# Weight sums moved from VectorE to GpSimd, and a maximum and exponential placed four half units sooner, in a fused attention and two-MLP kernel

## The chip, the cores and the metric

One core of one Trainium2 chip. The metric is the device time of one execution in microseconds; the kernel is compared by the median of its runs.

## The reference

`q`, `k`, `v` are (8, 8, 576, 64) in float32: eight batches, eight heads, 576 positions.

```python
q_s = exp(q - max(q, axis=-1)); q_s = q_s / (sum(q_s, axis=-1) + 1e-09)
k_s = exp(k - max(k, axis=2));  k_s = k_s / (sum(k_s, axis=2) + 1e-09)
x = q_s @ (k_s^T @ v)                       # per head, then (4608, 512)
x = relu(x @ w_in)**2 @ w_out               # 512 -> 2048 -> 512, weights float64
xn = x / sqrt(mean(x*x) + 1e-6) * rms_g
out = (silu(xn @ w_gate) * (xn @ w_val)) @ w_out2   # 512 -> 1536 -> 512
```

## The kernel before

The 4608 tokens are cut into nine blocks of 512. Every large product is done as three TensorE passes over a rounded high part and a low part of each operand (`PASSES`), so each operand is split: ACT writes the high part, VectorE (DVE) subtracts it from the value to get the low part.

**Stages.** A start stage handles the attention of the first two batches. Then a loop runs over units `(j, c)`: block `j` from 0 to 6 and `c` from 0 to 15, a slice of 128 of the 2048 hidden columns. One unit computes `ps_h` (12 matmuls, `p1_A`), its relu and square (ACT), its split `w` (`p1_hi`, `p1_lo`) and, two units later, the second product into `acc` (12 matmuls, `p1_B`). The last two blocks, and the second MLP, are done later by a scheme of seven products for eight (`PROD`, `BPROD`, `p2_A`, `p2_V`), which needs sums and differences of quarters of the weights.

**Side work in the loop.** Beside the matmuls, the units of blocks 2 to 6 carry three kinds of work:

- *Weights of the second MLP.* `tick` (line 454) runs a pipeline per weight piece: load of the float64 words (`raw`), ACT's conversion (`d_words`), three DVE instructions that build the float32 (`d_float`). When the four quarters of a piece are there, `d_quad` (line 415) makes the sums `s1`, `s2`, `s3`, `s4` of 128x512 (tiles `s` in the profile's rows, from `t11` to `t22`, there `t`), and queues seven splits `so` (`d_out`, line 398), which are stored to DRAM.
- *Sums of the first MLP's weights.* `d_light` (line 369) rebuilds two weights in float32 (tiles `t`), and makes four sums of 128x256 in place (`t<-t`), and queues two splits `so`. This is done 16 times, once in four units.
- *Attention of batches 2 to 7.* It goes by pairs of heads `hp` 0 to 3 of a batch `j`. Transposed k, `kT`, has **one** buffer (line 500). `a_loadk` loads it, `a_kmax` (line 562) takes its maximum on DVE (`mc`) and copies it out (`mcb`, one buffer), `a_kes` (line 571) takes its exponential on ACT for the sum alone, after which the buffer is free for the next pair's load. `a_kb` transposes `mcb` on TensorE (`ps_kb`, in one of two PSUM banks that the attention takes in turn, `a_ps`, line 102), `a_ksub` adds it to k (`kt`, DVE), `a_kexp` writes `ke` (ACT), `a_kv` multiplies it with v (`ps_kv`, TensorE).

**What sets the order.** In this stretch the instructions of DVE, ACT, GpSimd and TensorE stand in the order in which the code calls them (`pinned`). The steps of the attention have a place in half units: `FIRST` (line 1392) for even `hp`, `SECOND` (line 1396) for odd `hp`; pairs 0 and 1 share a base, pairs 2 and 3 one that lies 16 half units later. `a_kmax` and `a_kes` stand at 2 and 3 in `FIRST`, at 4 and 5 in `SECOND`. `SOONER` and `LATER` shift a whole batch's half. The DMA loads go through the queue of SyncE (SP); where they stand among each other is worked out by the framework.

The queued weight work is run at the end of each unit (line 1642): `sums_l` holds `d_light`'s sums and splits, `outs` holds `d_quad`'s sums and splits.

```python
for queue, n in ((sums_l, 2), (outs, 1 if ticks[0] > before else 3)):
    for _ in range(min(n, len(queue))):
        queue.pop(0)()
```

Of the kernel before, what the change touches and what calls it, by code (L numbers as in the profile page):

```python
# [8 lines left out]
F32 = mybir.dt.float32  # L9
# [31 lines left out]
def attention_moe_kernel(  # L41
# [14 lines left out]
    ve, se, ge, te = (  # L56
        InOrder(tc, engine, pinned) for engine in (nc.vector, nc.scalar, nc.gpsimd, nc.tensor)
    )
    B, H, S, D = q.shape
    NT, DM = out.shape  # L60
    P = 128
# [113 lines left out]
    pools = {}  # L175
# [23 lines left out]
    def flat(t):  # L199
        return t.rearrange("p b f -> p (b f)").bitcast(F32)  # L200
# [5 lines left out]
    def ahead(j, key):  # L206

        return j == 1 and key[0] == "i" and key[1] in AHEAD
# [56 lines left out]
    def used(key):  # L265
        if key not in res1:
            wt.pop(key)
            used_up[0] += 1
            feed()
# [55 lines left out]
    def send(key, t, after):  # L325
        late.append([after, key, t])
# [39 lines left out]
    outs, lows, sums_l = [], [], []  # L366
    halves_l = {}

    def d_light(kind, j, c):
        n, r = divmod(c, 2)  # L370
        if (kind, j) not in (("i", 2 + n % 2), ("o", 4 + n % 2)):
            return
        t = pools["d"].tile([P, 512], U32, tag=f"t{r}", name="t", bufs=1).bitcast(F32)
        w = wt[kind, c].bitcast(F32)
        ve.tensor_tensor(out=t, in0=w[:, 0], in1=w[:, 1], op=ALU.add)
        halves_l[r] = t
        if r == 0:
            return
        f = [halves_l.pop(0), halves_l.pop(1)]
        half = [f[0][:, 0:HF], f[0][:, HF:], f[1][:, 0:HF], f[1][:, HF:]]  # L380
        a11, a12, a21, a22 = half if kind == "i" else (half[0], half[2], half[1], half[3])

        def sub(out, in0, in1, op=ALU.subtract):
            sums_l.append(lambda: ve.tensor_tensor(out=out, in0=in0, in1=in1, op=op))

        sub(a22, a21, a22, ALU.add)
        sub(a21, a11, a21)
        sub(a11, a22, a11)
        if kind == "i":
            d_out(("L", kind, 1, n), lambda: f[1], sums_l)  # L390
            sub(a12, a12, a11)
            d_out(("L", kind, 0, n), lambda: f[0], sums_l)
        else:
            d_out(("L", kind, 0, n), lambda: f[0], sums_l)
            sub(a12, a12, a11)
            d_out(("L", kind, 1, n), lambda: f[1], sums_l)

    def d_out(key, f, outs=outs):
        def run():
            t = pools["q"].tile([P, 2, 512], F32R, tag="so", name="so", bufs=5)  # L400
            src = f().rearrange("p (g f) -> p g f", g=2)
            ts = t.rearrange("p g (a f) -> p g a f", a=2)
            se.activation(out=ts[:, :, 0], in_=src, func=AF.Copy)

            def low():
                ve.tensor_tensor(
                    out=ts[:, :, 1], in0=src, in1=ts[:, :, 0].bitcast(F32), op=ALU.subtract
                )
                send(key, t, 0)

            lows.append(low)

        outs.append(run)

    def d_quad(key):
        n, c = key
        if n != "11":
            return
        f = {"a" + b: floats.pop((b, c)) for b in ("11", "12", "21", "22")}

        def d_sum(name, in0, in1, op):
            def run():
                f[name] = pools["q"].tile([P, 512], F32, tag=name, name=name, bufs=1)
                ve.tensor_tensor(out=f[name], in0=f[in0], in1=f[in1], op=op)

            outs.append(run)

        def out(name):
            d_out((name, c), lambda: f[name])

        d_sum("s1", "a21", "a22", ALU.add)
        d_sum("s3", "a11", "a21", ALU.subtract)
        out("a22")
        d_sum("s2", "s1", "a11", ALU.subtract)
        out("a11")
        out("s1")
        out("s3")
        d_sum("s4", "a12", "s2", ALU.subtract)
        out("s2")
        out("a12")  # L440
        out("s4")

    due = {}
    for c in range(FF1):
# [7 lines left out]
    ticks = [0]  # L452
# [293 lines left out]
    def a_kvd_hi(j, hp):  # L746
        if j < B:
            split_hi(kvs, (j, hp), kvd[j % 2][hp // 2][:, hp % 2])

    def a_kvd_lo(j, hp):  # L750
        if j < B:
            split_lo(kvs, (j, hp))
            kvs.pop((j, hp))
# [170 lines left out]
    def p1_h(j, c):  # L924
        ps = ps_h.tile([P, T], F32, tag="h", name="ps_h")
        for kk in range(KD):
            mm3(ps, wl(("i", c), kk), lambda b: xts[j, kk][:, b, :], kk == 0, kk == KD - 1)
        return ps
# [14 lines left out]
    def p1_A(j, c):  # L943
        if not ahead(j, ("i", c)):
            kept[j, c] = p1_h(j, c)
            d_light("i", j, c)
            if not (j == 0 and ahead(1, ("i", c))):
                used(("i", c))
# [5 lines left out]
    def p1_ahead_r(c):  # L954
        p1_r(1, c)

    def p1_hi(j, c):
        if not ahead(j, ("i", c)):
            p1_r(j, c)
        r = kept.pop((j, c))  # L960
        ghl[1, j, c] = r
        split_hi(ghl, (1, j, c), g_tile(c % 4))

    def p1_lo(j, c):
        split_lo(ghl, (1, j, c))
# [440 lines left out]
    for j in range(2, NB):  # L1406
        for hp in range(NP):
            for n, (at, f) in enumerate(SECOND if hp % 2 else FIRST):
                at += (j - 1) * 2 * FF1 - 4 + 4 * FF1 // NP * (hp // 2)
                at += SOONER.get((j, hp // 2), 0)  # L1410
                if f in (a_loadk, a_loadq, a_loadv):
                    at += LATER.get((j, hp // 2), 0)
                    if j == NB - 1:
                        at = U0 + (5, 6, 7, 10)[hp]
                todo.setdefault(at, []).append((-n, j, hp, f))
# [34 lines left out]
    with ExitStack() as ctx_a:  # L1450
# [24 lines left out]
        for j in range(2):  # L1475
# [7 lines left out]
            out=neg_r, in0=ident, scalar1=-1.0, scalar2=0.0, op0=ALU.mult, op1=ALU.add  # L1483
# [104 lines left out]
        def attention(at):  # L1588
            for n, j, hp, f in todo.get(at, ()):
                f(j, hp)  # L1590
# [4 lines left out]
        for i, (j, c) in enumerate(units[: JU * FF1]):  # L1595
            if i < EARLY:
                continue
            if i == 2 * FF1:
                ctx_r.close()
                ctx_k.close()  # L1600
                pools["q"] = ctx_q.enter_context(
                    tc.tile_pool(name="qp", bufs=1, reuse_waits="tile")
                )
            if i == (JU - 1) * FF1 + 8:
                assert not outs and not sums_l and ticks[0] == len(jobs) + 3
                flush(all=True)
                ctx_q.close()
                ctx_d.close()
                pools["y"] = ctx.enter_context(
                    tc.tile_pool(name="by", bufs=1, reuse_waits="tile", side="right")  # L1610
                )
            if j == 0:
                unit_of_0(c)
                if 8 <= c < 8 + NP:
                    a_kvd_hi(1, c - 8)
                    a_kvd_lo(1, c - 8)
                attention(2 * i)
                attention(2 * i + 1)
                continue
            p1_A(j, c)  # L1620
            for x in last:
                p1_hi(*x)
            if ticks[0] > NJ1 + 4:
                flush()
            if c == LAG:
                p1_out(j - 1)
            attention(2 * i)
            pending.append((j, c))
            while beside:
                p1_ahead_r(beside.pop())  # L1630
            while len(pending) > (LAG + 1 if j > 0 and c == LAG else LAG):
                p1_B(*pending.pop(0))
            for x in last:
                p1_lo(*x)
            last = [(j, c)]
            if j == 1 and 4 <= c < 4 + NTAG:
                key = res1[c - 4]
                tc.keep_in_program_order(nc.sync.dma_start(out=wd[key], in_=flat(wt[key])))
            before = ticks[0]
            while ticks[0] < n_ticks(i):  # L1640
                tick()
            for queue, n in ((sums_l, 2), (outs, 1 if ticks[0] > before else 3)):
                for _ in range(min(n, len(queue))):
                    queue.pop(0)()
            attention(2 * i + 1)
            while lows:
                lows.pop(0)()
# [68 lines left out]
        for op in plan2:  # L1716
            at = None
            if op[0] == "A":
                _, s, n, q = op
                pinned[0] = True  # L1720
                p2_A(s, n, q)
                at = n * 2 * NS + q
                if at in A_SPLITS:
                    f, m = A_SPLITS[at]
# [4 lines left out]
            else:  # L1729
                _, s, i, n = op  # L1730
                at = i * NQ + n
# [73 lines left out]
```

## Time and profile before

| what | value |
|---|---|
| median of 3 runs (lowest to highest) | 1692.53 us (1690.88 to 1695.87) |
| the profiled execution's own time | 1696.69 us |
| its span, first to last instruction | 1694.9 us |
| busy PE / PEld / DVE / ACT / POOL, us | 1654.3 / 1367.1 / 1219.8 / 894.5 / 24.7 |
| mean granted TensorE clock | 0.992 |
| DMA | 434.08 MB, 256 GB/s |

PE is TensorE's matmuls, PEld its weight loads, which run beside them, POOL is GpSimd, SP is SyncE, whose queue issues the loads. "a<-b,c" is an instruction that writes tile a from b and c. All instructions that the kernel's own recording layer issues have line 34. In a row of a timeline, the bracket at the end says how long the engine sat idle before, and what ended that.

### The profile page before, as it was taken

How to read it: one execution, taken by the hardware profiler on the slowest of the kernel's cores; microseconds unless marked ns; L12 is line 12 of the kernel's file. 1: busy time of each engine (PE TensorE's matmuls, PEld its weight loads, DVE VectorE, ACT ScalarE, POOL GpSimd, SP SyncE). 2: the span in 40 equal slices, each digit the busy share in tenths (PEclk: the TensorE clock that was granted, in tenths of full speed). 3: DMA queues.
4: the chain of work that ended last, by engine and by line, in shares of the span. 5: the costliest groups of instructions: out<-in, count | busy, mean ns of one | idle time of the engine just before them, and what ended most of it. 6: DMA issues, size and time to landing. Idle time of an engine off the chain costs nothing.

```text
span 1694.9 us, 23168 instructions
## 1 busy us (share of the span) xinstructions
PE 1654.3 (98%) x8190; PEld 1367.1 (81%) x8190; DVE 1219.8 (72%) x1936; ACT 894.5 (53%) x1462; POOL 24.7 (1%) x39
## 2 busy tenths in 40 slices
PE   6999999999998999999999999999999999999999
PEld 4888888787777787888788888888888888888898
DVE  7985467778778788546775678667866786668666
ACT  7875456656655666458744444344444444424433
POOL 5000000000000000000000000000000000000000
PEclk9999999999999999999999999999999999999999
DMA  8876988999998997656668666866686658665898
GB/s 264 313 285 243 296 265 301 329 368 341 335 320 275 332 357 261 244 196 189 186 205 276 189 186 208 277 188 190 203 275 195 191 183 269 194 188 197 242 388 301
DMA packets 205410, 434.08 MB, mean 256 GB/s; under 512 B 60784, under 2 KB 97648, under 8 KB 204144
## 3 DMA queue, kind: packets, MB, share of 16 engines
q1 hardware_dynamic: 178272, 369.82, 67.3%
q10 hardware_dynamic: 27024, 62.79, 9.7%
q8 instruction: 66, 1.08, 0.3%
q14 instruction: 48, 0.39, 0.1%
HBM read 347.08 MB, written 85.46 MB: 255 GB/s over the span
## 4 chain that ended last, share of the span: by engine, by line
PE 81%; DVE 6%; DMA 6%; ACT 5%; issue 1%; ACTq 0%; POOL 0%; POOLq 0%; SPq 0%; DVEq 0%
PE ps_x L34 22%; PE ps_y L34 18%; PE acc L34 12%; PE ps_h L34 12%; PE ps_v L34 10%; PE ps_w L34 5%; DMA kT<-in_k_t 2%; DVE t L34 2%; DMA ws<-wd_i 1%; DVE so L34 1%; ACT r L34 1%; PE ps_kv L34 1%; DMA kt<-in_k 1%; PE ps_q L34 1%; DVE w L34 1%
## 5 line engine op out<-in xcount | busy, mean ns | idle before, releaser
L34 PE MATMUL acc<-w,ws 128*128 128x512 f32 x1008 | 251.5, 399 | 0.0
L34 PE MATMUL ps_h<-x,ws 128*128 128x512 f32 x1008 | 247.9, 397 | 0.0
L34 PEld LDWEIGHTS acc<-w,ws 128*128 128x128 f32 x1008 | 190.9, 192 | 40.8 <-DVE w L34 0.5
L34 PEld LDWEIGHTS ps_h<-x,ws 128*128 128x128 f32 x1008 | 189.2, 190 | 40.1 <-ACT r L34 0.3
L34 PE MATMUL ps_y<-xo,ws 128*128 128x512 f32 (+1 forms) x816 | 194.3, 373 | 0.3 <-ACT sa L34 0.3
L34 PE MATMUL ps_v<-xo,ws 128*128 128x512 f32 (+1 forms) x816 | 194.0, 373 | 0.0
L34 PE MATMUL ps_x<-ob,ws 128*128 128x512 f32 x768 | 177.4, 389 | 0.0
L34 PE MATMUL ps_x<-xo,ws 128*128 128x512 f32 (+1 forms) x720 | 168.9, 370 | 0.0
L34 PEld LDWEIGHTS ps_y<-xo,ws 128*128 128x128 f32 x816 | 145.0, 188 | 29.2 <-ACT sa L34 0.8
L34 PEld LDWEIGHTS ps_x<-ob,ws 128*128 128x128 f32 x768 | 144.1, 188 | 30.0
L34 PEld LDWEIGHTS ps_v<-xo,ws 128*128 128x128 f32 x816 | 144.9, 188 | 28.7
L34 DVE TENSOR_TENSOR u<-ps_y,p 128x512 f32<-128x512 f32 (+1 forms) x136 | 87.4, 643 | 104.8 <-PE ps_y L34 77.3
L34 ACT ACTIVATE ob<-gs 128x1024 fp32r<-128x1024 f32 (+1 forms) x105 | 102.2, 974 | 113.2 <-PE ps_x L34 52.1
L34 PEld LDWEIGHTS ps_x<-xo,ws 128*128 128x128 f32 x720 | 127.1, 188 | 24.4
L34 DVE TENSOR_TENSOR ob<-gs,ob 128x1024 fp32r<-128x1024 f32 (+1 forms) x105 | 116.5, 1111 | 30.1 <-ACT ob L34 29.6
L34 PE MATMUL ps_y<-ob,ws 128*128 128x512 f32 x576 | 133.9, 390 | 0.7 <-DVE ob L34 0.7
L34 ACT ACTIVATE p<-ps_x 128x512 f32<-128x512 f32 (+1 forms) x74 | 41.7, 564 | 174.1 <-PE ps_x L34 172.8
L34 PEld LDWEIGHTS ps_y<-ob,ws 128*128 128x128 f32 x576 | 107.9, 188 | 24.2 <-DVE ob L34 1.9
L34 DVE TENSOR_TENSOR w<-r,w 128x512 fp32r<-128x512 f32 x112 | 76.8, 686 | 46.8 <-ACT w L34 46.2
L34 PE MATMUL ps_w<-xo,ws 128*128 128x512 f32 (+1 forms) x408 | 97.1, 373 | 0.0
L34 ACT ACTIVATE silu<-silu 128x512 f32<-128x512 f32 (+1 forms) x90 | 49.4, 583 | 75.0 <-DVE silu L34 75.0
L34 ACT ACTIVATE r<-ps_h 128x512 f32<-128x512 f32 x112 | 65.9, 588 | 42.5 <-PE ps_h L34 41.2
(179 smaller groups left out, 2404.6 us busy)
## 6 DMA issues: line engine op xcount, KB each, us to landing
ws<-w_t SPq DMA_DIRECT2D x210, 512.0 KB, 3.7
ws<-wd_v SPq DMA_DIRECT2D x105, 512.0 KB, 3.4
ws<-wd_o SPq DMA_DIRECT2D x72, 512.0 KB, 5.9
ws<-wd_i SPq DMA_DIRECT2D x64, 512.0 KB, 5.7
w_t<-so ACTq DMA_DIRECT2D x42, 512.0 KB, 7.1
raw<-in_w_gv SPq DMA_DIRECT2D x36, 512.0 KB, 5.8
wd_v<-so ACTq DMA_DIRECT2D x21, 512.0 KB, 5.6
x<-x2d SPq DMA_DIRECT2D x9, 1024.0 KB, 7.4
```

What stands on the lines that cost most here:

```text
L34: ins = f(*args, **kw)
```

## The change

All sums of `d_light` and `d_quad` are issued on GpSimd (`ge`) at the moment when their operands are made, instead of on DVE from the two queues; the queues hold splits alone. Of `sums_l` at most one split is run per unit, and only one that was queued before the unit began (`old`); of `outs` one where the unit ticks or `sums_l` still holds something, else two. For batches 3 to 7 and even `hp`, `a_kmax` and `a_kes` stand four half units sooner.

```diff
@@ d_light
         def sub(out, in0, in1, op=ALU.subtract):
-            sums_l.append(lambda: ve.tensor_tensor(out=out, in0=in0, in1=in1, op=op))
+            ge.tensor_tensor(out=out, in0=in0, in1=in1, op=op)

         sub(a22, a21, a22, ALU.add)
         sub(a21, a11, a21)
         sub(a11, a22, a11)
-        if kind == "i":
-            d_out(("L", kind, 1, n), lambda: f[1], sums_l)
-            sub(a12, a12, a11)
-            d_out(("L", kind, 0, n), lambda: f[0], sums_l)
-        else:
-            d_out(("L", kind, 0, n), lambda: f[0], sums_l)
-            sub(a12, a12, a11)
-            d_out(("L", kind, 1, n), lambda: f[1], sums_l)
+        sub(a12, a12, a11)
+        for x in (1, 0) if kind == "i" else (0, 1):
+            d_out(("L", kind, x, n), lambda x=x: f[x], sums_l)
@@ d_quad
         def d_sum(name, in0, in1, op):
-            def run():
-                f[name] = pools["q"].tile([P, 512], F32, tag=name, name=name, bufs=1)
-                ve.tensor_tensor(out=f[name], in0=f[in0], in1=f[in1], op=op)
-
-            outs.append(run)
+            f[name] = pools["q"].tile([P, 512], F32, tag=name, name=name, bufs=1)
+            ge.tensor_tensor(out=f[name], in0=f[in0], in1=f[in1], op=op)
...
         d_sum("s1", "a21", "a22", ALU.add)
         d_sum("s3", "a11", "a21", ALU.subtract)
-        out("a22")
         d_sum("s2", "s1", "a11", ALU.subtract)
-        out("a11")
-        out("s1")
-        out("s3")
         d_sum("s4", "a12", "s2", ALU.subtract)
-        out("s2")
-        out("a12")
-        out("s4")
+        for name in ("a22", "a11", "s1", "s3", "s2", "a12", "s4"):
+            out(name)
@@ the table of the attention's places
                 at += SOONER.get((j, hp // 2), 0)
+                if j > 2 and hp % 2 == 0 and f in (a_kmax, a_kes):
+                    at -= 4
@@ the loop over units
+            old = min(1, len(sums_l))
             p1_A(j, c)
...
-            for queue, n in ((sums_l, 2), (outs, 1 if ticks[0] > before else 3)):
+            for queue, n in ((sums_l, old), (outs, 1 if ticks[0] > before or sums_l else 2)):
```

Two places show what moves. The first is SP's queue in batch 5, around the load of `kT` for its last pair (`hp` 3), which waits for the exponential of `hp` 2; `ws` are the loads of matmul weights that TensorE uses in turn (`wd_o_5`, `wd_i_8` and so on are their sources), `raw` and `qt` those of other side work. Before:

```order
L261 DMA ws_4664<-wd_o_5_108 128x1024
L527 DMA qt_4689<-in_q 48x2x256
L261 DMA ws_4705<-wd_i_8_109 128x1024
L281 DMA raw_4804<-in_w_gv 128x512
L261 DMA ws_4732<-wd_o_6_110 128x1024
L261 DMA ws_4770<-wd_i_9_111 128x1024
L501 DMA kT_4554<-in_k_t 128x576
L261 DMA ws_4793<-wd_o_7_112 128x1024
```

And with the change:

```order
L261 DMA ws_4670<-wd_o_5_108 128x1024
L488 DMA kT_4558<-in_k_t 128x576
L514 DMA qt_4697<-in_q 48x2x256
L261 DMA ws_4713<-wd_i_8_109 128x1024
L281 DMA raw_4813<-in_w_gv 128x512
L261 DMA ws_4740<-wd_o_6_110 128x1024
L261 DMA ws_4773<-wd_i_9_111 128x1024
L281 DMA raw_5020<-in_w_gv 128x512
L261 DMA ws_4794<-wd_o_7_112 128x1024
```

The load of `kT` now stands ahead of three loads of `ws`, and directly behind `wd_o_5`.

The second is DVE at the same pair: its maximum `mc`, and what stands behind it up to the split `x`, whose PSUM bank the next `ps_kb` takes. Before:

```order
L34 TENSOR_TENSOR t<-t 128x256
L34 TENSOR_TENSOR s_4809<-t_4514,t_4735 128x512
L34 TENSOR_REDUCE qm<-qt 128x8
L34 TENSOR_REDUCE mc<-kT 128x1
L34 COPY mcb<-mc 128x128
L34 TENSOR_TENSOR so<-t,so 128x2x256
L34 TENSOR_TENSOR qt<-qt,qm 128x512
L34 TENSOR_TENSOR kt<-kt,ps_kb 128x640
L34 TENSOR_TENSOR t<-ws 128x512
L34 TENSOR_TENSOR w<-r,w 128x512
L34 TENSOR_TENSOR s_4868<-t_4796,t_4514 128x512
L34 TENSOR_TENSOR s_4872<-s_4809,t_4796 128x512
```

Directly behind these stands `x<-ps_x,x`. With the change:

```order
L34 ISA t_4797<-t_4797,n 128x1024
L34 TENSOR_REDUCE qm<-qt 128x8
L34 TENSOR_REDUCE mc<-kT 128x1
L34 COPY mcb<-mc 128x128
L34 TENSOR_TENSOR so<-t,so 128x2x256
L34 TENSOR_TENSOR so<-t_4743,so 128x2x256
L34 TENSOR_TENSOR qt<-qt,qm 128x512
L34 TENSOR_TENSOR kt<-kt,ps_kb 128x640
L34 TENSOR_TENSOR t<-ws 128x512
L34 TENSOR_TENSOR w<-r,w 128x512
L34 TENSOR_TENSOR x<-ps_x,x 128x512
```

The four sums are gone from DVE here (two 128x512 of `s` and, ahead of `mc`, one `s` and one `t<-t`), and one more split `so` stands between `mcb` and `x`.

## Rows read from the trace of the kernel before

**Rows 1.** The page, part 1: busy time, share, instructions of each engine.

```profile
PE 1654.3 (98%) x8190; PEld 1367.1 (81%) x8190; DVE 1219.8 (72%) x1936; ACT 894.5 (53%) x1462; POOL 24.7 (1%) x39
```

**Rows 2.** One stretch: busy PE, PEld, DVE, ACT, POOL; clock; DMA share, GB/s.

```profile
300.00:670.00 370.00, 347.86 (x1808) 284.47 (x1807) 289.89 (x553) 231.09 (x416) 0.00 (x0) 0.96 0.92 326
```

**Rows 3.** Waits of PE, 300 to 670 us: total, times, longest.

```profile
PE ps_kb L34 <- DVE x L34: 12.0, 3, 4.9
PE ps_kv L34 <- ACT ke L34: 6.6, 3, 2.5
PE ps_x L34 <- DVE qT L34: 2.4, 2, 1.5
PE ps_kb L34 <- DVE qT L34: 0.9, 1, 0.9
PE ps_kb L34 <- DVE kt L34: 0.3, 1, 0.3
```

**Rows 4.** First of six stretches at low clock, and the sum of the six.

```profile
334.90:338.30 3.40, 3.40 (x9) 2.63 (x8) 3.35 (x8) 1.90 (x4) 0.00 (x0) 0.50 0.96 320
...
sum 27.20, PE 24.67 PEld 19.34 DVE 25.36 ACT 17.63 POOL 0.00; mean PE 4.11 PEld 3.22 DVE 4.23 ACT 2.94 POOL 0.00
```

**Rows 5.** Timeline of PE: start, duration, idle before. The first and longest such wait.

```profile
333.37 0.80 PE L34 MATMUL ps_kv<-vt,ke 128*64 128x64 f32 x20 [2.03 <-ACT ke L34]
...
469.74 0.45 PE L34 MATMUL ps_kb<-ident,mcb 128*128 128x128 f32 x1 [4.87 <-DVE x L34]
```

**Rows 6.** Tile mc, 210 to 670 us: waits before it; two of them, DVE's timeline.

```profile
  DMA kT<-in_k_t: 42.1, 10
...
375.23 0.75 DVE L34 TENSOR_REDUCE mc<-kT 128x1 f32<-128x576 f32 x1 [8.29 <-DMA kT<-in_k_t]
...
463.25 0.75 DVE L34 TENSOR_REDUCE mc<-kT 128x1 f32<-128x576 f32 x1 [2.55 <-DMA kT<-in_k_t]
```

**Rows 7.** Timeline of ACT and of SP's queue ahead of the first of these.

```profile
364.66 0.77 ACT L34 ACTIVATE kT<-kT,mc 128x576 f32<-128x576 f32 x1
...
368.86 0.40 SPq L501 DMA_DIRECT2D kT<-in_k_t  x1
```

**Rows 8.** Tile kT, whole span: its loads from issue to landing.

```profile
DMA to landing us min/median/max: 2.6/4.0/6.6
```

**Rows 9.** Timelines of DVE, SP and PE: two even maxima, a load, a transpose.

```profile
311.58 0.74 DVE L34 TENSOR_REDUCE mc<-kT 128x1 f32<-128x576 f32 x1
...
410.48 0.74 DVE L34 TENSOR_REDUCE mc<-kT 128x1 f32<-128x576 f32 x1
...
377.18 0.38 SPq L501 DMA_DIRECT2D kT<-in_k_t  x1
...
459.13 0.27 PE L34 MATMUL ps_kb<-ident,mcb 128*128 128x128 f32 x1
```

**Rows 10.** Groups of DVE by form: the sums that the change moves.

```profile
L34 DVE TENSOR_TENSOR t<-t 128x256 f32<-128x256 f32 x64 | 26.8, 419 | 0.5
...
L34 DVE TENSOR_TENSOR s<-t,t 128x512 f32<-128x512 f32 x18 | 12.1, 683 | 0.0
...
L34 DVE TENSOR_TENSOR s<-t,s 128x512 f32<-128x512 f32 x9 | 6.2, 684 | 0.0
L34 DVE TENSOR_TENSOR s<-s,t 128x512 f32<-128x512 f32 x9 | 6.1, 682 | 0.0
```

**Rows 11.** Groups of POOL by form: the two longest of its two-input instructions.

```profile
L34 POOL TENSOR_TENSOR x<-xf,x 128x512 fp32r<-128x512 f32 x4 | 5.1, 1284 | 0.0
L34 POOL TENSOR_TENSOR qt<-qt,qm 128x512 f32<-128x512 f32 x4 | 4.2, 1045 | 1.7 <-DVE qm L34 1.7
```

**Rows 12.** POOL and DVE at one time; all of that kind: least/median/most ns.

```profile
28.13 1.29 POOL L34 TENSOR_TENSOR x<-xf,x 128x512 fp32r<-128x512 f32 x1
...
28.40 1.30 DVE L34 TENSOR_SCALAR s<-raw 128x512 f32<-128x512 f32 x1
...
L34 DVE TENSOR_SCALAR s<-raw x16: 418/420/1298, 28.4 to 129.1; 128x512 f32<-128x512 f32 x16
```

## The prediction

> **What bounds the kernel now.** The first view is the page's table of busy time: TensorE is busy for 98% of the span, DVE for 72%, ACT for 53%, GpSimd for 1% [rows 1]. So only time in which TensorE waits, or runs at a low clock, can be won. The second view, busy time by stretch, shows where that is: the moved work and the attention of batches 3 to 7 lie at about 210 to 690 us, and between 300 and 670 us TensorE is busy for 347.9 of 370 us, at a mean granted clock of 0.96 [rows 2]. Idle there: 22.1 us.
>
> The third view, the waits, names what ended this idle time: three waits of ps_kb for DVE's split x, 12.0 us; three of ps_kv for ACT's ke, 6.6 us; and four smaller ones, 3.6 us [rows 3]. The fourth is the granted clock. After each of the six large waits the clock stands at 0.50, which is 1.2 of 2.4 GHz, for 3.4 or 6.8 us; the reader is to see in the first pair that the matmul that waited 2.03 us starts at 333.4 us and the low clock at 334.9 us [rows 4, 5]. After the smaller waits, the longest 1.5 us [rows 3], there is none. In these six stretches TensorE worked for 24.7 us at half speed [rows 4], which costs 24.7 / 2 = 12.3 us. Lost in all: 22.2 + 12.3 = 34.5 us, the most that the change can win.
>
> Fifth, what comes ahead of the large waits. On DVE the maximum mc of the odd pairs waits for the load of kT, ten times in batches 3 to 7, 42.1 us, at the worst 8.29 us; no even pair waits for it [rows 6]. This one wait holds DVE's whole queue: splits for TensorE, kt and x stand behind it. Its cause is the single buffer of kT: the load of the odd pair can only be issued after the exponential of the even pair (364.66 us, 0.77 us long), here at 368.86 us [rows 7], and takes 2.6 to 6.6 us to land [rows 8], while the odd maximum stands one half unit behind that exponential. The longest wait of TensorE is the plainest case: the odd maximum starts at 463.25 us after 2.55 us of idle time [rows 6], x stands eight places behind mcb, and ps_kb, which needs x's bank, starts at 469.74 us after 4.87 us [rows 5].
>
> **The change, part by part.**
>
> *The maximum and exponential of the even pairs, four half units sooner.* From one batch's first maximum (311.58 us) to the next one's (410.48 us) are 98.9 us [rows 9] and, by the tables of places, 30 half units, so 3.3 us each, and 13.2 us for four. The buffer is free that much sooner. On SP's queue the load moves past three loads of matmul weights, as the order shows, so that it can use this. The worst wait was 8.29 us, so each load should land some 5 us or more ahead of its maximum. The even loads lose 13.2 us of their lead: the load issued at 377.18 us has its maximum at 410.48 us [rows 9], and lands at the latest 6.6 us on, at 383.8, so 26 us ahead; 13 us are left. Nothing waits newly there. The even maximum itself moves into the tail of the pair before, which costs DVE the same 0.75 us and spares it in the thicker place.
>
> What is late next: mcb has one buffer, so the odd copy must wait for ps_kb of the even pair, which is not moved. In the case above that ran at 459.13 us [rows 9], ahead of 460.70, when the odd maximum could start without its wait; so nothing is left of that wait. Where TensorE comes later, up to some 3 us of DVE's wait stay, but then DVE is ahead of TensorE and waits for it.
>
> What TensorE's waits lose: in the longest case 2.55 us of the wait; between mcb and x two sums go and one split comes, one instruction of 0.6 us less; ahead of mc one s and one t<-t go, 0.95 us. 2.55 + 0.6 + 0.95 = 4.1 of 4.87 us, so 0.8 us stays, less than the waits that left the clock alone. The other five follow waits of DVE as long as their own or longer, and I take them as gone. Gain: 18.6 us of waits + 12.3 us of clock - 0.8 = 30.1 us. The four smaller waits (3.6 us) I leave: two are ps_x for qT, which is another chain.
>
> *The sums.* DVE loses 64 sums of 0.419 us (26.8 us) and 36 of 0.683 (12.1 + 6.2 + 6.1 us): 51.2 us [rows 10]. GpSimd gets them. Its own rows show 1.045 us for a 128x512 of this kind and 1.284 with a rounded output [rows 11]; a 128x256 it never ran. By DVE's ratio of the two sizes (419 / 683) it takes 0.64 us, an estimate; the bounds are 0.5 (half) and 1.045. That is 36 x 1.045 + 64 x 0.64 = 78.6 us over 480 us, on an engine that does nothing else there: its own time lies wholly beside other work. A chain of four takes 4.2 us, and the first split that needs a result is queued third, so ACT should not wait for it.
>
> But the two engines may hold each other up. The rows show one case: a DVE instruction of the kind that takes 0.420 us took 1.298 us, from 28.40 to 29.70, and GpSimd's instruction beside it ended at 29.42 [rows 12]; it looks as if DVE stood until then. No DVE instruction with two operands in SBUF ran beside GpSimd in this trace, so the price for the many of these (w, so, t, s) is unknown. Bounds: nothing, so 51.2 us less on DVE; or all of GpSimd's time, 78.6 - 51.2 = 27.4 us more (with the upper bound of a 128x256, 100 x 1.045 - 51.2 = 53.3 us more). The one case was a hold of 0.88 us for a GpSimd instruction of 1.29 us, but DVE is idle for a fifth of this stretch [rows 2] and has other kinds of instructions too; so I take half: 39.3 - 51.2, 11.9 us less. DVE then has less to do than before, but in pieces that hold it for a microsecond; I count this part as zero.
>
> The Trainium skill speaks against this part: by "SBUF — State Buffer", section "Who interferes with whom", a DVE instruction with two SBUF inputs contends with a GpSimd instruction that reads SBUF, and whoever is second stands still for the whole of the other. The one case in the rows agrees with such a hold; by the rule alone the full price would be due whenever they meet, which is the rival below.
>
> *The queues.* A unit now runs at most one split of each queue, or two of one; before, up to five entries. The number of splits is the same, so this only spreads work. Cost zero; its cover is ACT's idle time, 139 of 370 us [rows 2].
>
> **The sum.** The profiled execution took 1696.69 us: 1696.7 - 30.1 = 1666.6, so 1667 us. It lies 4.2 us above the median of the runs, 1692.53. I take nothing off for that: what differs between runs of before are waits of this kind, and what is left without them should be the same.
>
> **The rivals.** 0.3%, 5 us, is what a measurement of this kernel can tell from no change.
>
> *GpSimd's sums hold DVE in the thick places.* If they meet DVE's two-input instructions there, DVE is late again and half of the gain goes back: 1696.7 - 15 = 1682 us. For it: rows 12, and that the sums fall into the same units as before. Against it: DVE has 80 of 370 us to spare there [rows 2], and no longer waits 42 us for kT. 0.16.
>
> *GpSimd becomes DVE's brake, slower than before.* TensorE lost 30.9 us to 42.1 us of DVE's waits, 0.73 per microsecond. To eat up 30.1 us, DVE must lose 41 us net, so the 100 sums must hold it 51.2 + 41 = 92 us, 0.92 us each. That needs a 128x256 sum as dear as a 128x512, and a hold every time; then 53.3 x 0.73 = 39 us: 1666.6 + 39 = 1706 us. For it: the whole of a short instruction's fixed cost is unseen. Against it: DVE's ratio of sizes. 0.08.
>
> *The load comes no sooner.* If it is not the buffer but SP's own waits ahead of the load that set its time (365.4 to 368.9 us in the case shown [rows 7]), the waits only move with it, and it stays near 1692 us. Against it: the load now stands ahead of the three weight loads. 0.08.
>
> **How the numbers follow.** Main case 0.68, and faster by over 0.3% also in the first rival: 0.84. Within 0.3%: 0.08. Slower: 0.08. The least possible is 1696.7 - 34.5 = 1662.2 us; with a microsecond of scatter, 1661. The range reaches up past the first rival, to 1684.
>
> **What the profile will show.** Right: mc waits for kT fewer than three times from batch 3 on, TensorE's idle time in the stretch from 300 to 670 us is under 6 us, and the clock stays at 1.00 there. DVE's busy time falls by about 50 us where nothing holds it; where it is held, its two-input instructions show 1 us or more in place of 0.68, and GpSimd's show over 1.05 us. Wrong: ps_kb or ps_kv wait over 2 us with a low clock behind them, or SP waits for ACT's kT for long with loads of ws behind it.

## The result, and the profile after

On the first chip the changed kernel takes 1665.7 us (median of 4 runs, 1663.9 to 1668.1), before 1692.9 (4 runs): ratio 0.984, 95% interval 0.982 to 0.986. Forecast: 1667, range 1661 to 1684. In a later comparison on another chip the ratio was 0.986 (0.984 to 0.987), 1669.8 us.

The profiled execution took 1665.0 us, its span is 1662.9. Its busy time, from the page:

```profile
PE 1643.1 (99%) x8190; PEld 1360.8 (82%) x8190; DVE 1201.1 (72%) x1836; ACT 893.3 (54%) x1462; POOL 132.4 (8%) x139
```

Against [rows 1], GpSimd has 107.7 us more. DVE has 100 instructions less, but only 18.7 us, although these 100 took 51.2 us [rows 10].

The stretch with the matmuls of [rows 2] (counted in TensorE's order), now from 300 to 638.1 us, and what is left of low clock (columns as in those rows):

```profile
300.00:638.13 338.13, 335.90 (x1807) 277.31 (x1806) 270.18 (x463) 226.81 (x409) 89.49 (x83) 0.99 0.99 353
...
384.10:387.50 3.40, 3.40 (x16) 2.60 (x12) 3.22 (x8) 2.13 (x4) 1.90 (x3) 0.50 1.05 396
```

TensorE needs 338 instead of 370 us for the same matmuls, 32 us less, which is all that the execution won: it is idle for 2.2 instead of 22.1 us, and busy for 12.0 us less, since fewer matmuls ran at the low clock. One stretch of 3.4 us at 0.50, which is 1.2 GHz, is left of six. TensorE's waits from 205 to 680 us, which answer to [rows 3]:

```profile
PE ps_kv L34 <- ACT ke L34: 1.8, 1, 1.8
PE ps_kb L34 <- DVE x L34: 0.3, 1, 0.3
PE ps_x L34 <- DVE qT L34: 0.2, 1, 0.2
```

22.2 us have become 2.3. And what mc and its neighbours waited for, from the view of the tile (205 to 640 us; answers to the first of [rows 6]), with DVE's largest waits in the same stretch:

```profile
  PE ps_kb L34: 17.0, 8
  DMA ws<-wd_i: 3.5, 1
  DVE so L34: 3.3, 2
```

```profile
DVE so L34 <- ACT so L34: 28.0, 13, 6.2
DVE mcb L34 <- PE ps_kb L34: 17.0, 8, 4.6
DVE w L34 <- ACT w L34: 15.3, 19, 1.9
```

No wait for the load of kT is left from batch 3 on (ten before, 42.1 us). Two waits of DVE take its place: that of mcb for TensorE's transpose of the even pair, 17.0 us (0.5 before), and that of so for ACT, 28.0 us (15.0 before). TensorE loses next to nothing by them, as its 2.3 us show.

The order did what it says. SP's queue, the odd load of batch 5 directly behind its load of ws:

```profile
441.02 0.33 SPq L261 DMA_DIRECT2D ws<-wd_o  x1
441.66 0.33 SPq L488 DMA_DIRECT2D kT<-in_k_t  x1
```

The tightest pair is the last of batch 4. Its load is issued at 354.08 us, and the maximum starts at 363.98, with no idle time before it:

```profile
354.08 0.33 SPq L488 DMA_DIRECT2D kT<-in_k_t  x1
...
DMA to landing us min/median/max: 2.6/5.0/9.7
```

```profile
363.98 0.73 DVE L34 TENSOR_REDUCE mc<-kT 128x1 f32<-128x576 f32 x1
```

The last line of the first of these two is over all 24 loads of kT: the slowest, which is this one, took 9.7 us, before 6.6 [rows 8].

### The profile page after: what moved, and what is told of

It is laid out like the page before. It is cut to its first block, busy times and chain, and to the rows that moved or that the text cites. A ratio compares the mean times of both kernels' runs of the same rounds, so it can differ in the third digit from the quotient of the medians.

```text
span 1662.9 us, 23234 instructions
## 1 busy us (share of the span) xinstructions
PE 1643.1 (99%) x8190; PEld 1360.8 (82%) x8190; DVE 1201.1 (72%) x1836; ACT 893.3 (54%) x1462; POOL 132.4 (8%) x139
## 4 chain that ended last, share of the span: by engine, by line
PE 90%; DMA 4%; ACT 3%; DVE 2%; issue 1%; POOL 0%; SPq 0%; ACTq 0%; DVEq 0%; POOLq 0%
PE ps_x L34 22%; PE ps_y L34 19%; PE ps_h L34 16%; PE acc L34 16%; PE ps_v L34 10%; PE ps_w L34 5%; PE ps_kv L34 1%; DMA ws<-wd_o 1%; PE ps_q L34 1%; DMA w_t<-so 1%; ACT gu L34 1%; DMA wl_i<-so 1%; DMA vt<-in_v 0%; DMA ws<-w_t 0%; DMA raw<-in_w_gv 0%
## 5 line engine op out<-in xcount | busy, mean ns | idle before, releaser
L34 PE MATMUL acc<-w,ws 128*128 128x512 f32 x1008 | 245.5, 392 | 0.0
L34 PEld LDWEIGHTS acc<-w,ws 128*128 128x128 f32 x1008 | 187.0, 188 | 39.2 <-DVE w L34 0.2
L34 DVE TENSOR_TENSOR ob<-gs,ob 128x1024 fp32r<-128x1024 f32 (+1 forms) x105 | 116.6, 1111 | 30.1 <-ACT ob L34 29.6
L34 DVE TENSOR_TENSOR w<-r,w 128x512 fp32r<-128x512 f32 x112 | 80.8, 722 | 45.8 <-ACT w L34 45.5
```

Of the source, the lines that this page charges most:

```text
L34: ins = f(*args, **kw)
```

## The experiments

Each kernel ran beside the kernel before; ratios are to that, with the 95% interval. E1 to E4 shared a chip, E5 to E8 another, E9 to E12 a third; medians of before there: 1695.6, 1695.3, 1693.9 us.

**E1, the sooner places alone** (sums on DVE, in the old queues).

```diff
+                if j > 2 and hp % 2 == 0 and f in (a_kmax, a_kes):
+                    at -= 4
```

> The kernel before with one part of the change alone: the even pairs' maximum and exponential four half units sooner; all sums stay on DVE and in their queues. Theory (the single buffer of kT makes the odd maximum wait, that holds DVE, and DVE holds TensorE): mc waits for the load of kT at most twice from batch 3 on, TensorE's waits over 2 us fall from six to at most two, and the time is 1664 to 1674 us, most of the gain of 27 us. Rival (taking 51 us of sums off DVE is what frees TensorE): the time stays above 1682 us, less than 40% of the gain, though mc no longer waits.

1671.7 us, ratio 0.986 (0.983 to 0.988). No wait for kT from batch 3 on; the clock is not low from 100 us until the last 2 us, although one wait of 2.7 us is left. TensorE's waits, 205 to 680 us:

```profile
PE ps_x L34 <- DVE qT L34: 3.1, 4, 1.6
PE ps_kb L34 <- DVE x L34: 2.9, 2, 2.7
PE ps_kv L34 <- ACT ke L34: 1.6, 2, 1.2
PE ps_kb L34 <- DVE qT L34: 0.5, 1, 0.5
```

TensorE's waits fall from 22.2 to 8.1 us. So this one edit gives 24 us, nearly all.

**E2, everything but the sooner places.**

```diff
-                if j > 2 and hp % 2 == 0 and f in (a_kmax, a_kes):
-                    at -= 4
```

> The changed kernel without the sooner places: sums on GpSimd and splits paced as changed, the maximum and exponential of the even pairs where they stood before. Theory of the single buffer: mc waits for kT about ten times, 35 us or more in all, TensorE still waits over 2 us at least three times, 1680 to 1695 us. Rival of the sums: 1675 us or less.

1685.9 us, ratio 0.994 (0.992 to 0.997). The waits of mc (first line, from the tile's view) and the largest of TensorE's are there again:

```profile
  DMA kT<-in_k_t: 38.4, 9
```

```profile
PE ps_kb L34 <- DVE x L34: 10.4, 3, 4.9
PE ps_kv L34 <- ACT ke L34: 4.5, 2, 2.8
PE ps_kb L34 <- DVE kt L34: 1.2, 1, 1.2
```

The clock is low in two stretches, 10.2 us together (27.3 us in six before). A third of the gain comes without the sooner places; E5 asks from what.

**E3, all of the change, but every sum on DVE at the same place in the code.**

```diff
-            ge.tensor_tensor(out=out, in0=in0, in1=in1, op=op)
+            ve.tensor_tensor(out=out, in0=in0, in1=in1, op=op)
...
-            ge.tensor_tensor(out=f[name], in0=f[in0], in1=f[in1], op=op)
+            ve.tensor_tensor(out=f[name], in0=f[in0], in1=f[in1], op=op)
```

> The changed kernel with every sum at the same place in the code but issued on DVE instead of GpSimd. It tells the engine from the pace of the queues. If GpSimd's sums are worth about nothing to the time, because what DVE is spared it partly loses again to holds: within 4 us of the changed kernel, 1662 to 1670 us, with DVE's busy time about 20 us above it and no DVE instruction of two operands stretched over 0.75 us. Rival (GpSimd's sums matter): 1675 us or more, with TensorE waiting for DVE.

1667.8 us, ratio 0.983 (0.980 to 0.986). Its page:

```profile
PE 1640.7 (99%) x8190; PEld 1359.3 (82%) x8190; DVE 1222.9 (74%) x1936; ACT 893.0 (54%) x1462; POOL 24.7 (1%) x39
```

DVE is busy for 21.8 us more than in the changed kernel, none of its instructions is stretched (measured as in E6), and TensorE waits no more for it:

```profile
PE ps_kv L34 <- ACT ke L34: 1.9, 1, 1.9
PE ps_x L34 <- DVE qT L34: 0.5, 1, 0.5
```

**E4, two half units sooner instead of four.**

```diff
-                    at -= 4
+                    at -= 2
```

> The changed kernel with the even pairs' maximum and exponential two half units sooner instead of four, some 6.6 us. Theory of the single buffer: the buffer is free 6.6 us sooner than before, the worst waits of before were 8.3 and 6.2 us, so up to four waits of mc for kT of up to 2 us are left, TensorE waits over 2 us at most once, 1664 to 1672 us. Rival (it is not the buffer's time that counts): no step between before and four half units, so close to the time without any shift.

1667.9 us, ratio 0.984 (0.981 to 0.987). mc waits for kT four times, at most 3.3 us (2 had been expected), TensorE over 2 us once (2.45 us, with no low clock behind it). Half of the shift already gives the gain, though the margin is used up.

**E5, the queues' pace alone**: E3 without the sooner places.

> The queues' new pace alone: every sum on DVE at once where the code makes it, one split per queue and unit, and the even pairs' maximum where it stood before. The run with sums on GpSimd but without the sooner places was 9.7 us faster than before. Theory (that gain is the pace's, GpSimd is worth nothing): the same gain within 5 us, 1681 to 1691 us on a chip where before takes 1692 to 1696. Rival (the gain is GpSimd's): within 4 us of before.

1687.1 us, ratio 0.995 (0.994 to 0.997). As E2, as far as the intervals tell: so the third that E2 showed is the pace's (sums at once, splits one by one), not GpSimd's. mc waits ten times for kT, 34.7 us, the clock is low in four stretches, 20.5 us together, and TensorE's largest waits, 205 to 680 us, are

```profile
PE ps_kb L34 <- DVE x L34: 12.9, 3, 5.6
PE ps_kv L34 <- ACT ke L34: 5.2, 2, 3.1
```

**E6, the 36 large sums twice on GpSimd.**

```diff
             ge.tensor_tensor(out=f[name], in0=f[in0], in1=f[in1], op=op)
+            ge.tensor_tensor(out=f[name], in0=f[in0], in1=f[in1], op=op)
```

> The changed kernel with each of the 36 sums of 128x512 issued twice on GpSimd, with the same result: the price of GpSimd's time to DVE. In the changed kernel 108 us of GpSimd's sums stretched 41 DVE instructions by 26.5 us in all. Theory (a hold in proportion to GpSimd's time that reads SBUF, and DVE has room for it): 45 to 60 us more on GpSimd, 10 to 18 us more stretch on DVE, time 1664 to 1670 us. Rival (GpSimd is DVE's brake): 1675 us or more, TensorE waits over 2 us again.

The 26.5 us that are named there are worked out: the DVE instructions after 60 us of the span that took over 60 ns longer than the median of their form before, summed over what they took longer.

1681.0 us, ratio 0.991 (0.989 to 0.993). The changed kernel did not run on this chip; by its two ratios, 0.984 and 0.986, this one is 9 to 13 us slower. The theory was wrong on the size, and the rival came true. The page, and TensorE's largest waits, 205 to 680 us:

```profile
PE 1646.8 (98%) x8190; PEld 1363.1 (81%) x8190; DVE 1229.7 (73%) x1836; ACT 893.3 (53%) x1462; POOL 189.2 (11%) x175
```

```profile
PE ps_x L34 <- DVE qT L34: 4.4, 2, 3.9
PE ps_kv L34 <- ACT ke L34: 3.3, 2, 2.1
```

56.8 us more on GpSimd make DVE busy for 28.6 us more, with the same work; 10 to 18 had been expected. The clock is low in three stretches of 3.4 us.

**E7, three fills ahead of each of these sums instead**, which read nothing.

```diff
+            for _ in range(3):
+                ge.memset(f[name], 0.0)
             ge.tensor_tensor(out=f[name], in0=f[in0], in1=f[in1], op=op)
```

> The changed kernel with three fills with zero of the same tile ahead of each of the 36 sums on GpSimd: GpSimd is busy longer, but the added instructions read nothing. Theory (DVE is held by GpSimd's reads): the stretch of DVE's instructions stays at 22 to 31 us though GpSimd is busy for 40 us or more longer. Rival (any GpSimd instruction on SBUF holds DVE): stretch of 38 us or more. Time in both 1663 to 1672 us.

1670.8 us, ratio 0.986 (0.984 to 0.988). GpSimd's page time is 182.3 us, 49.9 more than in the changed kernel, and DVE's 1205.4, only 4.3 more. Measured as in E6, the stretch is 31.0 us, at the edge of what was expected of reads; what grew are small instructions with one input. One of them stood through a sum and the fill behind it (DVE's and GpSimd's timeline):

```profile
508.42 1.71 DVE L34 TENSOR_SCALAR qs<-qs 128x8 f32<-128x8 f32 x1
```

```profile
508.36 1.29 POOL L34 TENSOR_TENSOR s<-s,t 128x512 f32<-128x512 f32 x1
509.59 1.70 POOL L34 MEMSET s<- 128x512 f32 x3
```

Such an instruction takes 0.17 us undisturbed. The first fill ends at 510.11 us, the DVE instruction at 510.14. So it looks as if a fill too holds some DVE instructions, but the many with two inputs were stretched no more than in the changed kernel.

**E8, the stores' issue on ACT behind the attention's steps.** The wait of 1.8 us that is left was traced to ACT: it stood for 4.5 us around the issue of two stores that waited for loads of ws, with ke behind them.

```diff
-            if ticks[0] > NJ1 + 4:
-                flush()
             if c == LAG:
                 p1_out(j - 1)
             attention(2 * i)
+            if ticks[0] > NJ1 + 4:
+                flush()
```

> The changed kernel with the issue of the weight stores on ACT moved behind the attention's steps of the first half unit. In the changed kernel the largest wait left is ps_kv for ke, 1.8 us at 382 us, with a low clock behind it: ACT stood for 4.5 us at the issue of a store that waited for a load of ws. Theory (that wait is the last large one): it goes, 1661 to 1666 us, no low clock before the end. Rival (the wait of the store holds what now stands behind it): 1665 to 1672 us, with another wait of TensorE for ACT.

1663.1 us, ratio 0.981 (0.978 to 0.983). After 290 us, TensorE's waits in the loop shrink to one of 0.25 us, and the only low clock ahead of the end is 3.4 us at 41 us, ahead of this code. But on this evidence the step from the changed kernel was not clear.

**E9 to E12, four kernels on one chip.**

> The changed kernel once more, on one chip with the three that follow, in five rounds, to tell differences of some microseconds. Theory: 0.983 to 0.985 of before.

> All of the change with every sum on DVE at the same place in the code. Theory (the move to GpSimd is worth nothing to the time): within 3 us of the changed kernel either way. Rival (GpSimd's part is worth a few microseconds): 4 us or more slower than it.

> The changed kernel with the stores' issue on ACT behind the attention's steps. Theory: 1 to 5 us faster than the changed kernel, no wait of TensorE over 1 us after 100 us of the span. Rival: the same within 1 us, since the wait of 1.8 us with its low clock is not in every execution.

> Both: stores' issue later and every sum on DVE. Theory: within 2 us of the same with the sums on GpSimd, 1660 to 1666 us where before takes 1692. Rival (DVE with all sums is near its limit): 4 us or more slower, with TensorE waiting for DVE.

| kernel | median us | ratio to before (95%) |
|---|---|---|
| E9, the changed kernel | 1669.8 | 0.986 (0.984 to 0.987) |
| E10, all sums on DVE | 1667.8 | 0.985 (0.983 to 0.987) |
| E11, E9 with the stores later | 1662.2 | 0.981 (0.980 to 0.983) |
| E12, E10 with the stores later | 1665.1 | 0.983 (0.981 to 0.984) |

E9 and E10 are within 3 us of each other, as the theory had it. E11 is faster than the changed kernel by 7.6 us, with intervals that do not meet: more than the 1 to 5 expected. The wait that it removes was longer in E9, 3.35 us with 6.8 us of low clock. Some 1.7 us between the two profiled executions is not the edit's: E9's had 3.4 us of low clock at 41 us, ahead of this code, E11's had not. ACT's timeline in E9 and TensorE's behind it:

```profile
382.25 0.37 ACTq L34 DMA_DIRECT2D wl_i<-so  x1
384.61 0.52 ACTq L34 DMA_DIRECT2D w_t<-so  x1
385.18 0.74 ACT L34 ACTIVATE ke<-kt 128x640 f32<-128x640 f32 x1 [5.93 <-DMA ws<-wd_o]
```

```profile
385.97 1.34 PE L34 MATMUL ps_kv<-vt,ke 128*64 128x64 f32 x20 [3.35 <-ACT ke L34]
```

And ACT's in E11:

```profile
378.98 0.73 ACT L34 ACTIVATE ke<-kt 128x640 f32<-128x640 f32 x1
383.74 0.37 ACTq L34 DMA_DIRECT2D wl_i<-so  x1
384.66 0.53 ACTq L34 DMA_DIRECT2D w_t<-so  x1
385.23 0.63 ACT L34 ACTIVATE so<-s 128x512 fp32r<-128x512 f32 x1 [5.52 <-DMA kt<-in_k]
```

ACT stands as long, but ke is out by then, and TensorE does not wait for what stands behind. E12 is between the two: with the sums on DVE it is 2.9 us slower than E11, where 2 had been expected at most; the intervals do not quite tell them apart.

## Why the prediction was right

**What bounds the kernel: right, but for one of the six waits.** With the even pairs' maximum sooner, and nothing else, TensorE's waits fell from 22.2 to 8.1 us and the low clock went, 24 us (E1). Without it DVE's waits for kT stay, whatever is done with the sums (38.4 us in E2, 34.7 in E5), and TensorE's mostly, 16.8 and 19.9 us. That it is the one buffer, and not where the maximum stands on DVE, is supported by E4, where the waits come back in part at half the shift; a second buffer for kT was not tried.

Five of the six large waits are gone. The second one stayed, before the same matmul (kernel before, then the change):

```profile
388.06 0.80 PE L34 MATMUL ps_kv<-vt,ke 128*64 128x64 f32 x20 [2.09 <-ACT ke L34]
```

```profile
383.50 0.87 PE L34 MATMUL ps_kv<-vt,ke 128*64 128x64 f32 x20 [1.79 <-ACT ke L34]
```

"The other five follow waits of DVE ... and I take them as gone" failed here: once DVE is in time, ACT is late with ke at this place, since it stands at the stores (E8).

**The clock: it came back, but not by the rule that the sum used.** Six stretches at 1.2 GHz became one, and TensorE's busy time fell by 12.0 us, where 12.3 had been counted. But the prediction read from one trace that a low clock follows waits of 2 us and more, and not waits of up to 1.5 us. In the changed kernel the clock fell 0.6 us after the matmul that had waited 1.79 us started; waits of 2.45 us (E4), 2.67 (E1), 2.78 (E2) and 3.10 us (E5) had no low clock behind them. The last of these, and the 10 us from its matmul on:

```profile
389.36 0.80 PE L34 MATMUL ps_kv<-vt,ke 128*64 128x64 f32 x20 [3.10 <-ACT ke L34]
```

```profile
389.36:399.36 10.00, 10.00 (x63) 8.32 (x64) 7.30 (x18) 5.30 (x11) 0.00 (x0) 1.00 0.94 307
```

So the length of a wait alone does not tell whether the clock falls; what else decides was not tried.

**The sum: right in total, in part by luck.** 30.1 us were forecast against the profiled execution; it is 31.7 us, 1696.7 - 1665.0 (27.2 us between the medians; the profiled execution of before lay 3.8 us above its median). I had 3.6 us of small waits stay and 0.8 us of the longest; both went nearly whole, but the 1.8 us of the second wait and one low clock are there.

**How far the loads land ahead: wrong, without harm.** "Each load should land some 5 us or more ahead of its maximum" took the landing time from before, 6.6 us at most. Loads of kT now take up to 9.7 us; why they take longer was not tried. Of the ten odd loads five landed 6 us or more ahead of their maximum, and three 0.2 to 1.0 us. E4 shows that some waits of 3 us can be borne.

**The sums, counted as zero: right, with two terms mis-sized that cancel.** GpSimd's time: 78.6 us forecast, 107.7 measured. Its groups:

```profile
L34 POOL TENSOR_TENSOR t<-t 128x256 f32<-128x256 f32 x64 | 53.2, 831 | 397.2 <-DVE t L34 350.5 <-DVE rk L34 40.1 <-ACT r L34 2.8
L34 POOL TENSOR_TENSOR s<-t,t 128x512 f32<-128x512 f32 x18 | 25.6, 1420 | 96.2 <-DVE t L34 83.7 <-ACT n L34 4.7 <-DVE rk L34 4.5
```

I took 1.045 us from a row whose second operand is one value spread over 64 columns; the other row, 1.284 us with two full operands, was the nearer one. The 128x256 sums, put at 0.64 us, take 0.83 in the mean. What lies above GpSimd's shortest times I take for holds by DVE, which is not shown one by one. What this took from DVE: 39.3 us forecast (half of 78.6), 32.5 measured (51.2 - 18.7; 29.4 against E3), about 30% of GpSimd's time. The rows that were missing before exist now; a DVE instruction with two operands in SBUF, 0.68 us alone, beside a sum that ended at 345.65 us (DVE, then GpSimd):

```profile
344.72 1.47 DVE L34 TENSOR_TENSOR so<-t,so 128x512 fp32r<-128x512 f32 x1
```

```profile
344.35 1.30 POOL L34 TENSOR_TENSOR s<-t,t 128x512 f32<-128x512 f32 x1 [5.95 <-DVE t L34]
```

Over the run, so<-t,so went from 0.682 to 0.880 us in the mean, on 59 instructions. That is what "SBUF — State Buffer", section "Who interferes with whom", of the Trainium skill states: two SBUF inputs meet GpSimd's reads, and the second stands still. By the same section an instruction of GpSimd that only writes SBUF does not contend with DVE's two-input instructions, but can contend with a tensor_scalar that uses both ports. E7 agrees with the first half, and there it was a tensor_scalar that stood; whether it used both ports no run shows. As far as E3 and E10 tell, the result was zero since both sides, 18.7 us net, lie under DVE's spare time once it no longer waits for kT.

**The queues' pace, "cost zero": this step failed.** Alone it gives 8 us (E5), the same as with the sums on GpSimd (E2, 10 us). My cover was ACT's idle time, and beyond the longest wait I had not asked what the new order does to DVE's chains. What the 8 us are made of is shown in part: in E5 TensorE's waits are 19.9 us against 22.2, and the low clock is 20.5 us against 27.3. The three waits for x are no shorter there (12.9 us against 12.0), so a shorter chain between mcb and x does not show; why the others shrink stays open. Beside the sooner places little of it is left: E1 and the changed kernel differ by less than their intervals.

**The rivals.** None came. The brake of GpSimd is real, though: E6 shows it at work, with 56.8 us more on GpSimd, 9 to 13 us of the gain gone. At 108 us DVE still had room.

## What to carry to other kernels

Where a wait of one engine stands in front of everything that another needs, look for the buffer that makes it: here a step moved by 13 us, with a load that it frees, was worth 24 of 27 us, and the 51 us of work taken off the waiting engine nothing that could be measured. Work moved to GpSimd is not taken off VectorE for free: price it with a row that has full operands, and count holds back (here 30% of the first 108 us, half of the next 57). Put what can wait at its issue, such as a store, behind what others wait for.

## What the runs showed that was not expected

- ACT stood for 4.5 and 5.9 us around the issue of two stores that waited for loads of ws to land, in the changed kernel and in E9. The semaphores in the traces say why: each of the two stores signals on the semaphore that such a load used before it, and an instruction ahead of the store waits for that load (in the changed kernel the loads landed at 380.03 and 382.00 us, the stores were issued at 380.11 and 382.08). So it is the program that makes them wait.
- GpSimd's sums of 128x512 with two full operands took 1.28 us at the least, and s<-s,t 1.65 us in the mean (1.31 in E7), so it looks as if both engines pay.
- A DVE instruction of 0.17 us stood 1.71 us behind two of GpSimd (E7).
